# A fused recurrent-attention and two-MoE kernel: low parts of the weights formed on the tensor engine, two-operand GpSimd work moved to the vector engine

## The chip, the cores and the metric

The kernel runs on one core of a Trainium2 chip. A core has five engines that run side by side and wait for each other through semaphores: TensorE (PE in the rows; its weight loads are PEld), VectorE (DVE), ScalarE (ACT), GpSimd (POOL) and SyncE (SP), which only issues transfers here. The metric is the device time of one execution in microseconds, the median of the timed runs. The kernel before took 1139.43 us (three runs, 1137.97 to 1142.35).

## The reference, cut to what matters

```
for t in range(768):                       # 4 batches x 8 heads, state 40 x 40
    y[t]  = r[t] @ state
    Sa    = state @ a[t]
    state = state * w[t] - outer(Sa, b[t]) + outer(v[t], k[t])
x = y as 3072 rows of 320                  # 8 heads x 40
h = x @ w_in                               # 320 -> 2048
g = h if h >= 1, 0 if h <= -1, else (h + 1)**2 / 4
x = g @ w_out                              # 2048 -> 320
h = max(x @ w1, x @ w2, x @ w3)            # 320 -> 768
out = h @ w_out2                           # 768 -> 320
```

The MoE weights arrive as 64-bit floats. The kernel builds a 32-bit float from the two 32-bit words of each, and then splits it into a high part H, rounded to the tensor engine's fast format (fp32r), and a low part L = value - H. The activations are split the same way, so that one product is three fast products: H times H, H times L, L times H.

## The kernel before, in words

**Stages.** The recurrence runs in 24 chunks of 32 time steps over all 32 (batch, head) pairs. `prep` makes, for two chunks at once, running products X of the decay and their reciprocals R, and `front` and `back` work one chunk: scale k, b and a by R and X (tiles KBT and ta), build small triangular matrices LM and invert them (tiles lp, itmp, T, ttr, a long series of small VectorE instructions), solve for U, and update the state Z. Z of one chunk is needed by the next. After every second chunk, `moe1` runs one unit of the first MoE: 256 rows of x through 128 products with w_in (line 810) and 96 with w_out (line 833), with an activation tile q and its parts gH and gL between them. A last stage, `moe2`, runs the second MoE (lines 947 and 973) when the recurrence has ended.

**Weights.** `weights1` brings the weights of the first MoE in 26 pieces through four raw buffers (`raw0` to `raw2` and `raw4`). `narrow` (715 to 719) turns 64 into 32 bits: ScalarE scales the high word into a tile `tmp` and takes its sign, VectorE shifts the low word (717) and joins both (718), and GpSimd or VectorE multiplies by the sign (719). `split` copies H on ScalarE (737) and subtracts on VectorE or GpSimd (738). The tiles `tmp` are the two q tiles of the MoE and one more. gH, gL and the second pair of x tiles are given the place of the raw buffers by `gates` (762 to 769), which comes when the pieces are done. The second MoE's weights are narrowed between the chunks (`pieces`) and kept in DRAM until `phase2` splits them.

**Order.** Nothing is ordered by hand. Every step is a task with one or more engines it may run on and a duration in ns for each. `Plan.run` puts the tasks on the engines by priority, along a clock of its own made of these durations, and the instructions are written out in that order; each engine then runs its queue strictly in order. Where a task names two engines, the one that would finish it first in the plan, with a constant added for each engine (1500 ns for VectorE, 0 for GpSimd), gets it. Where the plan leaves TensorE without work, `emit` writes products nobody reads (lines 359 and 1000, here called fillers) into a free PSUM bank.

Of the kernel before, what the change touches and what calls it, by code (L numbers as in the profile page):

```python
# [244 lines left out]
def dve(n):  # L245
    return 68 + n / 0.96
# [6 lines left out]
def pool(n):  # L253
    return 98 + n * 2.2
# [11 lines left out]
class Kernel:  # L266
# [46 lines left out]
    def setup_attn(self):  # L313
# [5 lines left out]
        self.mask = ap.tile([128, 7, 32], F32, name="mask")  # L319
        self.delta = ap.tile([128, 4], F32, name="delta")  # L320
# [46 lines left out]
    def prep(self, p):  # L367
# [9 lines left out]
        eng = lambda n: (("DVE", dve(n)),) if p == 0 else (("POOL", 720.0 if n == 128 else pool(n)), ("DVE", dve(n)))  # L377
        P.add((("POOL", 400.0), ("DVE", 150.0)) if p else (("DVE", 150.0),), lambda e: self.copy(e, blk(X, 0), blk(wt, 0)), r=wk, w=xk)
# [4 lines left out]
        P.add((("POOL", 330.0), ("DVE", 120.0)) if p else (("DVE", 120.0),), lambda e: self.copy(e, cum[:, :, 0:3], X[:, :, 8:25:8]), r=xk, w=ck)  # L383
# [58 lines left out]
    def front(self, c):  # L442
# [7 lines left out]
        RX = (("POOL", pool(1024)), ("DVE", dve(1024))) if c > 1 else (("DVE", dve(1024)),)  # L450
        AX_ = (("POOL", pool(512)), ("DVE", dve(512))) if c > 1 else (("DVE", dve(512)),)
# [52 lines left out]
        def op(n, fn, r, w):  # L504
            P.add((("DVE", dve(n) + 100),), fn, r=r, w=w)
# [186 lines left out]
    def setup_moe1(self):  # L692
# [15 lines left out]
    def narrow(self, raw, tmp, n, rk, tk):  # L708
# [31 lines left out]
    def weights1(self):  # L740
# [49 lines left out]
    def moe1(self, u):  # L790
# [6 lines left out]
        for mp in range(8):  # L797
# [23 lines left out]
            P.add((("POOL", pool(512)), ("DVE", dve(512)))[u == 11:], lambda e, q=q, j=j: self.tt(e, self.gL[j], q, self.gH[j].bitcast(F32), ALU.subtract),  # L821
# [54 lines left out]
    def phase2(self):  # L876
# [6 lines left out]
        for k, (_, n) in enumerate(self.pieces2):  # L883
# [3 lines left out]
            if k < 18:  # L887
# [4 lines left out]
                if kt < 2:  # L892
                    P.add((("DVE", dve(n)), ("POOL", pool(n))), lambda e, src=src, j=j, kt=kt, cs=cs: self.tt(e, tl["w3"][:, j, 2 + kt, cs], src(), tl["w3"][:, j, kt, cs].bitcast(F32), ALU.subtract),
                          r=[("tmp2", i), ("w3", j, kt, x)], w=[("w3", j, 2 + kt, x)])
                else:
                    P.add((("DVE", dve(n)), ("POOL", pool(n))), lambda e, src=src, j=j, cs=cs: self.tt(e, tl["w3"][64:128, j, 4, cs], src()[64:128], tl["w3"][64:128, j, 4, cs].bitcast(F32), ALU.subtract),
                          r=[("tmp2", i)], w=[("w3", j, 4, x)])
            else:
                m = k - 18
                P.add((("ACT", act(n)),), lambda e, src=src, m=m: self.copy(e, tl["wo2"][:, m, 0], src()), r=[("tmp2", i)], w=[("wo2", m, 0)])  # L900
                P.add((("DVE", dve(n)), ("POOL", pool(n))), lambda e, src=src, m=m: self.tt(e, tl["wo2"][:, m, 1], src(), tl["wo2"][:, m, 0].bitcast(F32), ALU.subtract),
# [287 lines left out]
def constants():  # L1189
# [9 lines left out]
        "ident": np.eye(128, dtype=np.float32),  # L1199
        "mask": np.stack([lower, two(k, b), two(k, b), lower, two(b, k), two(b, k), two(k, k)], 1),  # L1200
# [54 lines left out]
```

## Time and profile before

| | us |
|---|---|
| median of three runs | 1139.43 (1137.97 to 1142.35) |
| the profiled execution, device time | 1135.63 |
| its span, first to last instruction | 1133.8 |
| TensorE busy in the span | 1050.0 |
| VectorE busy | 660.7 |
| ScalarE busy | 489.4 |
| GpSimd busy | 435.7 |

The span has four stretches: the start, in which the weights come in and the first two chunks run (0 to 127 us); the chunks with the first MoE's units between them (127 to about 840); a short passage; and the second MoE (from 860 on). Busy time of TensorE is modelled for pipelined products and says little about how near it is to its best. A duration of a VectorE row reaches from its start to its end and can overlap the next by some 0.08 us.

### The profile page before, as it was taken

The numbers are of one execution on the slowest core, as the hardware profiler recorded it, in microseconds if no ns is written. First come the engines' busy times: TensorE is split into PE (matmuls) and PEld (weight loads), VectorE is DVE, ScalarE is ACT, GpSimd is POOL, SyncE is SP. The second block draws the span as 40 slices with busy tenths as digits, with TensorE's granted clock in tenths as the row PEclk, the third lists the DMA queues.
The fourth block names the chain that finished last, engine by engine and source line by source line (L and its number), as shares of the span: only waits on it lengthen the run. The fifth ranks groups of instructions, "written<-read, shape, count | busy, mean of one in ns | idle before, by whom it ended". The sixth has DMA issues, their size and how long they took to land.

```text
span 1133.8 us, 50184 instructions
## 1 busy us (share of the span) xinstructions
PE 1050.0 (93%) x22708; PEld 948.5 (84%) x22708; DVE 660.7 (58%) x1509; ACT 489.4 (43%) x1137; POOL 435.7 (38%) x478
## 2 busy tenths in 40 slices
PE   6888799999999999998999989999999999999996
PEld 6877789888888888887888878888998888888885
DVE  7989968576684939577483938555244333332321
ACT  3465355545554444544445353445564212222121
POOL 4979642356654545355545525522134000000000
PEclk9799899899999999999999999999999999999998
DMA  8444231313332222322121211200053101100000
GB/s 221 126 142 124 85 107 49 95 54 92 99 90 84 76 76 56 103 60 75 51 59 31 55 43 36 62 26 24 4 157 111 40 12 52 34 18 24 1 24 27
DMA packets 42866, 76.66 MB, mean 68 GB/s; under 512 B 8820, under 2 KB 24436, under 8 KB 42644
## 3 DMA queue, kind: packets, MB, share of 16 engines
q1 hardware_dynamic: 42500, 73.31, 22.9%
q8 instruction: 180, 2.95, 1.1%
q14 instruction: 42, 0.34, 0.1%
q10 hardware_dynamic: 144, 0.07, 0.0%
HBM read 60.96 MB, written 12.39 MB: 65 GB/s over the span
## 4 chain that ended last, share of the span: by engine, by line
PE 75%; DVE 11%; ACT 4%; issue 4%; DMA 4%; POOL 0%; SPq 0%; DVEq 0%; ACTq 0%; POOLq 0%
PE bank L947 18%; PE bank L810 15%; PE bank L833 12%; PE bank L973 6%; PE bank L1000 5%; PE bank L585 3%; PE bank L562 3%; PE bank L577 2%; DVE Z L301 2%; PE bank L666 2%; PE bank L479 2%; PE bank L432 2%; PE bank L652 2%; DMA KBT<-in_kbT 2%; ACT VU L289 1%
## 5 line engine op out<-in xcount | busy, mean ns | idle before, releaser
L833 PE MATMUL bank<-wo,gH 128*128 128x320 f32 x768 | 181.7, 323 | 0.0
L810 PE MATMUL bank<-xH,wi 128*128 128x256 f32 x960 | 160.7, 298 | 1.1 <-issue 1.1
L301 POOL TENSOR_TENSOR gL<-q,gH 128x512 fp32r<-128x512 f32 x86 | 110.8, 1291 | 123.5 <-ACT gH L281 92.9
L817 ACT ACTIVATE q<-bank,half 128x512 f32<-128x512 f32 x96 | 66.0, 688 | 165.8 <-PE bank L810 154.5
L810 PEld LDWEIGHTS bank<-xH,wi 128*128 128x128 f32 x960 | 131.4, 195 | 5.3 <-issue 1.3
L819 DVE SCALAR_TENSOR_TENSOR q<-bank,q 128x512 f32<-128x512 f32 x96 | 65.8, 685 | 107.8 <-ACT q L818 88.8
L833 PEld LDWEIGHTS bank<-wo,gH 128*128 128x128 f32 x768 | 125.3, 191 | 2.7
L833 PE MATMUL bank<-wo,gL 128*128 128x320 f32 x384 | 119.5, 311 | 0.0
L810 PE MATMUL bank<-xL,wi 128*128 128x256 f32 x576 | 103.0, 288 | 7.5 <-DVE xL L301 4.6
L947 PE MATMUL bank<-wi,w 128*128 128x512 f32 x432 | 102.7, 396 | 0.0
L1000 PE MATMUL bank<-ident 128*128 128x128 bf16 (+2 forms) x1194 | 88.3, 233 | 9.1 <-DVE LM L301 6.7
L947 PEld LDWEIGHTS bank<-wi,w 128*128 128x128 f32 x432 | 80.8, 188 | 18.6
L810 PEld LDWEIGHTS bank<-xL,wi 128*128 128x128 f32 x576 | 84.9, 196 | 8.6 <-DVE xL L301 5.4
L1000 PEld LDWEIGHTS <-ident 128*128 128x128 bf16 x1194 | 77.6, 102 | 13.8 <-issue 9.2
L301 DVE TENSOR_TENSOR q<-s,bank 128x512 f32<-128x512 f32 x36 | 24.8, 688 | 83.8 <-PE bank L947 83.1
L833 PEld LDWEIGHTS bank<-wo,gL 128*128 128x128 f32 x384 | 73.0, 190 | 0.1
L281 ACT CAST gH<-q 128x512 fp32r<-128x512 f32 x96 | 59.0, 615 | 27.7 <-PE bank L833 20.0
L947 PE MATMUL bank<-yH,w 128*128 128x512 f32 x270 | 70.5, 391 | 0.4 <-DVE wi L301 0.4
L281 ACT CAST wi<-s 128x512 fp32r<-128x512 f32 x36 | 22.5, 625 | 109.0 <-DVE s L301 109.0
L973 PE MATMUL bank<-wo,wi 128*128 128x320 f32 x432 | 66.0, 309 | 0.0
L973 PEld LDWEIGHTS bank<-wo,wi 128*128 128x128 f32 x432 | 64.7, 188 | 1.4
L301 POOL TENSOR_TENSOR R<-R,wT 104x128 f32<-104x128 f32 x74 | 56.1, 759 | 19.1 <-DVE R L388 5.7
(145 smaller groups left out, 2057.1 us busy)
## 6 DMA issues: line engine op xcount, KB each, us to landing
KBT<-in_kbT SPq DMA_DIRECT2D x24, 416.0 KB
raw<-in_moe_w_out SPq DMA_DIRECT2D x22, 320.0 KB
VU<-in_vn SPq DMA_DIRECT2D x96, 64.0 KB
wT<-in_wT SPq DMA_DIRECT2D x12, 429.0 KB
ta<-in_aT SPq DMA_DIRECT2D x24, 208.0 KB
tr<-in_rT SPq DMA_DIRECT2D x24, 208.0 KB
raw<-in_moe_w SPq DMA_DIRECT2D x12, 384.0 KB
raw<-in_moe_w_in SPq DMA_DIRECT2D x8, 512.0 KB
```

The lines of the kernel that those rows point to most:

```text
L281: self.nc.scalar.copy(out, in_)
L301: (self.nc.vector if eng == "DVE" else self.nc.gpsimd).tensor_tensor(*a)
L432: nc.tensor.transpose(p[:, m * 104:(m + 1) * 104], src(m), self.ident[0:104, 0:104])
L562: nc.tensor.matmul(self.bank[gs[x].bank][ts, o + j * D:o + (j + 1) * D], t[lo:hi, j, ts], z(lo, hi, bb, j), start=(opens and j == 0), stop ...
L585: nc.tensor.matmul(self.bank[g1[q].bank][us, o:o + D], self.ttr[QS[bb], h].rearrange("p i q -> p (i q)"), ru[QS[bb], h, :], start=(first a ...
L810: nc.tensor.matmul(p, a, b, start=(i == 0), stop=(i == 7))
L817: P.add((("ACT", act(512)),), lambda e, q=q, bv=bv: nc.scalar.activation(q, bv(), AF.Relu, bias=self.half, scale=0.5), w=[("q", j)], g=[g])
L819: P.add((("DVE", dve(512)),), lambda e, q=q, bv=bv: nc.vector.scalar_tensor_tensor(q, bv(), 1.0, q, ALU.max, ALU.min), w=[("q", j)], g=[g])
L833: nc.tensor.matmul(p, a, b, start=(m == 0 and i == 0), stop=(m == 15 and i == 2))
L947: nc.tensor.matmul(p, a, b, start=(i == 0), stop=(i == 7))
L973: nc.tensor.matmul(p, a, b, start=(m == n == 0), stop=(m == 5 and n == 2))
L1000: nc.tensor.matmul(self.bank[b][:, 0:n], w[:, 0:128], w[:, 0:n], start=True, stop=True)
```

## The change

- `split` no longer subtracts. A new function `rest` lets TensorE add the value times the identity and H times minus the identity in a PSUM bank of class "h" (banks 4 and 5, which the first MoE's units use later), and ScalarE copies the sum to L. The constant minus1 is one more input, loaded on ScalarE's queue ahead of ident.
- `narrow` writes to three tiles of their own; q is no longer used for it, gH and gL have their place from the beginning, and `gates` (now `others`) only makes the second x tiles. In exchange there are two raw buffers and raw4 instead of three and raw4.
- All two-operand work that could go to GpSimd is now VectorE's alone: X, R and their copies in `prep`, KBT and ta in `front`, the sign product in `narrow`, gL in `moe1`, the low parts in `phase2`. GpSimd keeps the constant on lp's diagonal, copies of WCT, and the squares of q where the plan gives them to it.
- Two durations of the plan change: the small steps of the inversion from +100 to +20 ns, the shift in `narrow` from +250 to +0.

```
-        eng = lambda n: (("DVE", dve(n)),) if p == 0 else (("POOL", 720.0 if n == 128 else pool(n)), ("DVE", dve(n)))
+        eng = lambda n: (("DVE", dve(n)),)
...
-        RX = (("POOL", pool(1024)), ("DVE", dve(1024))) if c > 1 else (("DVE", dve(1024)),)
-        AX_ = (("POOL", pool(512)), ("DVE", dve(512))) if c > 1 else (("DVE", dve(512)),)
+        RX = (("DVE", dve(1024)),)
+        AX_ = (("DVE", dve(512)),)
...
-            P.add((("DVE", dve(n) + 100),), fn, r=r, w=w)
+            P.add((("DVE", dve(n) + 20),), fn, r=r, w=w)
...
+        self.gH, self.gL = (t([128, 2, 256], n, 2, F32R) for n in ("gH", "gL"))
...
-        self.raw = [rp.tile([128, 1024], F32, name=f"raw{i}") for i in range(3)]
-        self.tmp = [x.rearrange("p a b -> p (a b)") for x in self.q] + [rp.tile([128, 512], F32, name="tmp")]
+        self.raw = [rp.tile([128, 1024], F32, name=f"raw{i}") for i in range(2)]
+        self.tmp = [rp.tile([128, 512], F32, name=f"tmp{i}") for i in range(3)]
...
-        P.add((("DVE", dvc(n) + 250),), lambda e: nc.vector.tensor_scalar(lo, lo, 29, None, ALU.logical_shift_right), w=rk)
+        P.add((("DVE", dvc(n)),), lambda e: nc.vector.tensor_scalar(lo, lo, 29, None, ALU.logical_shift_right), w=rk)
...
-        P.add((("POOL", pool(n)), ("DVE", dve(n))), lambda e: self.tt(e, tmp, tmp, sg, ALU.mult), r=rk, w=[tk])
+        P.add((("DVE", dve(n)),), lambda e: self.tt(e, tmp, tmp, sg, ALU.mult), r=rk, w=[tk])
...
-        P.add((("DVE", dve(n)), ("POOL", pool(n))), lambda e: self.tt(e, L_, st, H_.bitcast(F32), ALU.subtract), r=[sk, hk], w=[lk])
+        self.rest(st, H_, L_, n, [sk, hk], lk)
+
+    def rest(self, st, H_, L_, n, rk, lk):
+        nc, P = self.nc, self.P
+        g = Group("h")
+        def diff(e):
+            p = self.bank[g.bank][0:128, 0:n]
+            nc.tensor.matmul(p, self.ident, st, start=True, stop=False)
+            nc.tensor.matmul(p, self.minus1, H_.bitcast(F32), start=False, stop=True)
+        P.add((("PE", n * 3.6),), diff, r=rk, g=[g], k=8)
+        P.add((("ACT", act(n)),), lambda e: self.copy(e, L_, self.bank[g.bank][:, 0:n]), w=[lk], g=[g])
...
-            P.add((("POOL", pool(512)), ("DVE", dve(512)))[u == 11:], lambda e, q=q, j=j: self.tt(e, self.gL[j], q, self.gH[j].bitcast(F32), ALU.subtract),
+            P.add((("DVE", dve(512)),), lambda e, q=q, j=j: self.tt(e, self.gL[j], q, self.gH[j].bitcast(F32), ALU.subtract),
```

The order of VectorE in the middle of the recurrence, from the transposition that ends one chunk's inversion (ttr) to the state update (Z). Before:

```order
L534 STREAM_TRANSPOSE ttr_139<-T_136 128x32x8
L301 TENSOR_TENSOR gL_2431<-q_83,gH_2429 128x512
L717 TENSOR_SCALAR raw_142<-raw_142 128x384
L718 SCALAR_TENSOR_TENSOR raw_142<-raw_142 128x384
L301 TENSOR_TENSOR Z_128<-bank_67,Z_128 104x2x4x40
L301 TENSOR_TENSOR Z_128<-bank_68,Z_128 104x2x4x40
L301 TENSOR_TENSOR Z_128<-Z_128,WCT_130 104x2x4x40 x2
L819 SCALAR_TENSOR_TENSOR q_82<-bank_71,q_82 128x512
```

The same stretch of VectorE's queue, of a like pair of chunks, in the changed kernel:

```order
L301 TENSOR_TENSOR ta_122<-ta_122,X_114 104x512
L301 TENSOR_TENSOR R_116<-R_116,wT_112 104x128
L301 TENSOR_TENSOR raw_149<-raw_149 128x384
L536 STREAM_TRANSPOSE ttr_146<-T_143 128x32x8
L396 TENSOR_REDUCE lim_148<-cum_118 104x1 x2
L301 TENSOR_TENSOR KBT_120<-KBT_120,R_116 104x1024
L301 TENSOR_TENSOR gL_87<-q_83,gH_85 128x512
L301 TENSOR_TENSOR Z_135<-bank_67,Z_135 104x2x4x40
L301 TENSOR_TENSOR Z_135<-bank_70,Z_135 104x2x4x40
L301 TENSOR_TENSOR Z_135<-Z_135,WCT_137 104x2x4x40 x2
L834 SCALAR_TENSOR_TENSOR q_82<-bank_72,q_82 128x512
```

The products of ta, R, raw and KBT, which stood on GpSimd, now stand in VectorE's queue; those of ta and KBT follow a transfer. Between the transposition of lp of chunk 4 and that of chunk 6 VectorE had 103 instructions and has 140; up to that of chunk 2 it had 196 and has 231.

TensorE in the start, around the transposition of VU and the state product (KBn) of the first chunk. Before:

```order
L652 MATMUL bank_69<-ident,VU_123 128x128 x4
L652 MATMUL bank_70<-ident,VU_123 128x128 x4
L1000 LDWEIGHTS ident
L1000 MATMUL bank_71<-ident 128x128
...
L634 MATMUL bank_69<-VU_123,KBn_119 40x40
L634 MATMUL bank_70<-VU_123,KBn_119 40x40
```

The same place in the changed kernel:

```order
L654 MATMUL bank_68<-ident,VU_130 128x128 x4
L654 MATMUL bank_67<-ident,VU_130 128x128 x4
L750 MATMUL bank_72<-tmp_93,ident 128x320
L751 MATMUL bank_72<-wo_79,minus_106 128x320
L636 MATMUL bank_68<-VU_130,KBn_126 40x40
L636 MATMUL bank_67<-VU_130,KBn_126 40x40
```

The two products of a piece's low part stand where 31 fillers stood. Ahead of the first product of the first MoE there were 982 fillers and are 332, and all but a few of the 24 low parts; from there to the second MoE there were 212 fillers of 256 columns and are 84, and 4 short ones.

## Rows read from the trace of the kernel before

**Rows 1.** Busy time by stretch: TensorE, its loads, VectorE, ScalarE, GpSimd, granted clock, DMA, GB/s
```profile
0.00:127.00 127.00, 98.95 (x2749) 91.95 (x2749) 115.86 (x213) 60.51 (x139) 94.91 (x104) 0.88 0.55 151
150.00:810.00 660.00, 615.60 (x17823) 561.52 (x17821) 421.70 (x1072) 325.20 (x794) 300.94 (x332) 0.98 0.23 64
810.00:860.00 50.00, 49.38 (x469) 46.47 (x468) 22.18 (x36) 31.02 (x62) 19.04 (x18) 1.00 0.44 129
860.00:1134.00 274.00, 263.08 (x1327) 226.99 (x1325) 81.88 (x123) 61.72 (x118) 6.99 (x8) 0.99 0.10 28
```

**Rows 2.** The chain that ended last, shares of the span by engine
```profile
PE 75%; DVE 11%; ACT 4%; issue 4%; DMA 4%; POOL 0%; SPq 0%; DVEq 0%; ACTq 0%; POOLq 0%
```

**Rows 3.** VectorE's groups by form: busy us, mean ns of one, idle before
```profile
L301 DVE TENSOR_TENSOR Z<-Z,WCT 104x320 f32<-104x320 f32 x46 | 39.8, 895 | 0.0
L301 DVE TENSOR_TENSOR Z<-bank,Z 104x320 f32<-104x320 f32 x46 | 20.6, 481 | 34.2 <-PE bank L634 32.0 <-ACT raw L716 2.3
L526 DVE TENSOR_TENSOR itmp<-T,lp 128x16 f32<-128x16 f32 (+1 forms) x144 | 52.9, 405 | 0.3
L529 DVE TENSOR_REDUCE ir<-itmp 128x4 f32<-128x16 f32 (+1 forms) x144 | 26.9, 222 | 0.0
L530 DVE TENSOR_TENSOR itmp<-ir,lp 128x16 f32<-128x16 f32 (+1 forms) x144 | 44.1, 340 | 0.0
L510 DVE TENSOR_TENSOR itmp<-lp 128x16 f32<-128x16 f32 x24 | 14.4, 598 | 0.3
```

**Rows 4.** Timeline of VectorE and GpSimd at 118 us: start us, us
```profile
118.19 3.48 DVE L718 SCALAR_TENSOR_TENSOR q<-q,raw 128x320 uint32<-128x320 uint32 x2
118.73 2.58 POOL L301 TENSOR_TENSOR KBT<-KBT,R 104x1024 f32<-104x1024 f32 x1
```

**Rows 5.** VectorE's own price of moved forms: tile gL (min/median/max ns), timeline of the start
```profile
L301 DVE TENSOR_TENSOR gL<-q,gH x10: 678/692/2415, 400.0 to 856.2; 128x512 fp32r<-128x512 f32 x10
...
6.05 2.98 DVE L301 TENSOR_TENSOR X<-X,wT 104x128 f32<-104x128 f32 x7
...
19.90 0.38 DVE L301 TENSOR_TENSOR R<-R,wT 104x128 f32<-104x128 f32 x1
20.20 0.48 DVE L718 SCALAR_TENSOR_TENSOR q<-q,raw 128x320 uint32<-128x320 uint32 x1
```

**Rows 6.** The chain in order of time, dense stretches: start us, us
```profile
451.85 0.94 PE bank L810 x8
452.79 0.71 PE bank L562 x57
453.50 1.14 PE bank L810 x8
...
477.99 1.07 PE bank L666 x64
...
829.48 3.52 PE bank L833 x24
833.00 2.83 PE bank L810 x24
```

**Rows 7.** VectorE's timeline: the transposition of lp of chunks 2 and 22
```profile
115.78 2.00 DVE L492 STREAM_TRANSPOSE lp<-LM 128x1024 f32<-128x1024 f32 x1
...
746.51 2.04 DVE L492 STREAM_TRANSPOSE lp<-LM 128x1024 f32<-128x1024 f32 x1
```

**Rows 8.** The chain: a transfer and fillers in the start, products of line 810 at 216
```profile
17.64 8.49 DMA raw<-in_moe_w_out
...
42.51 16.13 PE bank L1000 x263
...
216.04 2.01 PE bank L810 x8
```

**Rows 9.** Who waited for whom: us in total, times, longest
```profile
DVE q L819 <- ACT q L818: 88.8, 43, 6.5
POOL ta L301 <- DMA ta<-in_aT: 52.9, 14, 7.5
DVE LM L301 <- PE bank L479: 32.3, 9, 7.3
DVE Z L301 <- PE bank L634: 32.0, 11, 5.5
POOL KBT L301 <- DMA KBT<-in_kbT: 22.1, 7, 7.9
```

More of the change, by code (lines that the diff above doesn't have):

```diff
@@ L376, in prep @@
         blk = lambda t, i: t[:, :, i:i + 25:8]
-        eng = lambda n: (("DVE", dve(n)),) if p == 0 else (("POOL", 720.0 if n == 128 else pool(n)), ("DVE", dve(n)))
-        P.add((("POOL", 400.0), ("DVE", 150.0)) if p else (("DVE", 150.0),), lambda e: self.copy(e, blk(X, 0), blk(wt, 0)), r=wk, w=xk)
+        eng = lambda n: (("DVE", dve(n)),)
+        P.add((("DVE", 150.0),), lambda e: self.copy(e, blk(X, 0), blk(wt, 0)), r=wk, w=xk)
         for i in range(1, 8):
@@ L382, in prep @@
             P.add(eng(256), lambda e, k=k: self.tt(e, X[:, :, k:k + 8], X[:, :, k:k + 8], X[:, :, k - 1:k].to_broadcast([104, 32, 8]), ALU.mult), w=xk)
-        P.add((("POOL", 330.0), ("DVE", 120.0)) if p else (("DVE", 120.0),), lambda e: self.copy(e, cum[:, :, 0:3], X[:, :, 8:25:8]), r=xk, w=ck)
+        P.add((("DVE", 120.0),), lambda e: self.copy(e, cum[:, :, 0:3], X[:, :, 8:25:8]), r=xk, w=ck)
         P.add(eng(32), lambda e: self.tt(e, cum[:, :, 3:4], X[:, :, 31:32], wt[:, :, 32:33], ALU.mult), r=wk + xk, w=ck)
@@ L401, in pieces @@
             for rows, src in srcs:
-                P.add((("SP", 450.0),), lambda e, rows=rows, src=src, n=n: nc.sync.dma_start(flat.bitcast(U32)[rows, 0:2 * n], src.bitcast(U32)), w=[("raw", 3)], size=1024 * n)
-            self.narrow(flat[:, 0:2 * n], flat[:, 768:768 + n], n, [("raw", 3)], "flat")
-            P.add((("SP", 450.0),), lambda e, k=k, n=n: nc.sync.dma_start(self.w2d[k][:, 0:n], flat[:, 768:768 + n]), r=[("raw", 3), "flat"], w=[("w2d", k)], size=512 * n)
+                P.add((("SP", 450.0),), lambda e, rows=rows, src=src, n=n: nc.sync.dma_start(flat.bitcast(U32)[rows, 0:2 * n], src.bitcast(U32)), w=[("raw", 2)], size=1024 * n)
+            self.narrow(flat[:, 0:2 * n], flat[:, 768:768 + n], n, [("raw", 2)], "flat")
+            P.add((("SP", 450.0),), lambda e, k=k, n=n: nc.sync.dma_start(self.w2d[k][:, 0:n], flat[:, 768:768 + n]), r=[("raw", 2), "flat"], w=[("w2d", k)], size=512 * n)
     def slot(self, h):
@@ L760, in weights1, with others @@
                 self.split(io["moe_w_out"][m * 128:(m + 1) * 128, :], DM, wo[:, m, 0], wo[:, m, 1], ("wo", m, 0), ("wo", m, 1))
-        P.add((("SP", 1.0),), lambda e: self.gates(), w=[("raw", i) for i in range(3)] + ["tmp"] + [(n, j) for n in ("gH", "gL") for j in range(2)] + [(n, 1, c) for n in ("xH", "xL") for c in range(2)])
-    def gates(self):
+        P.add((("SP", 1.0),), lambda e: self.others(), w=[("raw", i) for i in range(2)] + [("tmp", i) for i in range(3)] + [(n, 1, c) for n in ("xH", "xL") for c in range(2)])
+    def others(self):
         self.rctx.close()
-        gp = self.ctx.enter_context(self.tc.tile_pool(name="gates", bufs=1, side="right"))
-        self.gH, self.gL = ([gp.tile([128, 2, 256], F32R, name=f"{n}{i}") for i in range(2)] for n in ("gH", "gL"))
+        gp = self.ctx.enter_context(self.tc.tile_pool(name="others", bufs=1, side="right"))
         for x, n in ((self.xH, "xH1"), (self.xL, "xL1")):
@@ L900, in phase2 @@
                 P.add((("ACT", act(n)),), lambda e, src=src, m=m: self.copy(e, tl["wo2"][:, m, 0], src()), r=[("tmp2", i)], w=[("wo2", m, 0)])
[L901 removed]
+                P.add((("DVE", dve(n)),), lambda e, src=src, m=m: self.tt(e, tl["wo2"][:, m, 1], src(), tl["wo2"][:, m, 0].bitcast(F32), ALU.subtract),
                       r=[("tmp2", i), ("wo2", m, 0)], w=[("wo2", m, 1)])
```

13 lines of the change are left out of this document (8 added, 5 removed).

## The prediction

> **What bounds the kernel now.** I read the busy times by stretch first, then the chain of waits, then VectorE's groups by form, and last the chain in order of time.
>
> By stretch [rows 1] there are three regimes. In the start VectorE is busy 115.86 of 127 us and sets the pace. From 150 to 810 TensorE is busy 615.60 of 660, though modelled, with VectorE at 421.70. After 860 TensorE never stops, and VectorE is at 81.88 of 274. The chain [rows 2] is TensorE for 75% and VectorE for 11%, some 125 us of the 1133.8.
>
> VectorE's groups [rows 3] show what part of that is not work. The update of Z with both operands in SBUF takes 895 ns on average, the one of the same size with an operand in PSUM 481. Line 526 takes 405 ns, line 529, which reduces what 526 has just written, 222. The reduction has one operand, the product two. The timeline shows why [rows 4]: two joins of line 718, for which 0.48 us apiece is normal [rows 5], lasted 3.48 us while GpSimd ran one product of 2.58 us. A two-operand instruction of VectorE is held up by one of GpSimd. Four groups [rows 3] give a lower bound for it: 46 x (895 - 481) = 19.0 us, 144 x (405 - 222) = 26.4, 144 x (340 - 222) = 17.0, 24 x (598 - 222) = 9.0, together 71 us. The joins and the other small lines come on top; I take 90 us over the 810 us in which GpSimd works.
>
> In the middle two chunks and a unit of the first MoE take (746.51 - 115.78) / 10 = 63.1 us [rows 7]; I call this a pair. TensorE's own need in one, from dense stretches of the chain [rows 6]: 128 products of line 810 at 2.83 / 24 = 0.118 us and 96 of line 833 at 3.52 / 24 = 0.147 make 29.2; the bursts of a chunk (some 16, of 0.71 to 1.07 for the products with small tiles, the transpositions less) add up to about 12.1, so 24.2 for two; and a block of eight of line 810 behind a burst takes 1.14 instead of 0.94, so 0.2 for each of some 26 blocks, 5.2. Sum 58.6. The remaining 4.5 us of a pair are waits and fillers; that is all the middle can give, 10.5 pairs x 4.5 = 47 us.
>
> **The change part by part.** The sum stands against the profiled execution, 1135.6 us; the median of the runs is 3.8 higher, so the forecast of the median is moved by that.
>
> *GpSimd's work on VectorE.* It removes the 90 us of holding up and adds the work itself. A pair gets 140 - 103 = 37 instructions more. Prices [rows 5]: gL at 512 columns 0.69 us; X, seven in 2.98, so 0.43 each when each waits for the last; R 0.38, after which the next starts at 0.30. So 37 instructions cost 11 (at 0.30) to 25 us (at 0.69); most are X and R, so I take 0.45 and 17 us. VectorE in a pair: 421.70 / 660 x 63.1 = 40.3 now, less 90 x 63.1 / 810 = 7, plus 17: 50 of 63. It stays below TensorE's 58.6.
>
> [...]
>
> *The middle.* With the holding up gone, Z, the inversion and gL (two engine changes less) come when the plan has them. VectorE keeps 13 us of slack in a pair, and will at times still be late, so I give back 3.5 of the 4.5 us: 10.5 x 3.5 = 37 us. Bounds: 47 (all), and below zero the rival of VectorE's queue. That only 88 fillers stand there instead of 212 is part of this, not a further term.
>
> *The start.* GpSimd is busier here, 94.91 of 127 against 300.94 of 660 [rows 1], so of the 90 us I put 90 x 87 / (87 + 192) = 28 here, each stretch's VectorE time weighted by GpSimd's share. VectorE gets 231 - 196 = 35 instructions more, at 0.45 some 16 us. Net 12 us earlier. Bounds: 28 earlier (what is added is hidden), 42 later (the third rival below).
>
> *Low parts on TensorE.* 24 pieces, 8 of 512 and 16 of 320 columns, two products each. The trace has no full fp32 product of this shape. From below: the fast format's 0.147 us for 320 columns [rows 6], so 8 x 2 x 0.235 + 16 x 2 x 0.147 = 8.5 us. From above: the 3.6 ns per column that the diff gives the plan, 8 x 1.84 + 16 x 1.15 = 33 us. In the same stretch 650 fillers go, at 16.13 / 263 = 0.061 us [rows 8] 40 us. So it costs nothing while the pieces are there in time; if not, the whole queue of TensorE stands behind the product, since it takes its work in order. ScalarE gets 24 copies of at most 0.7 us, 17 us, and is busy only 60.51 of 127.
>
> *Own tiles.* gH, gL and q no longer wait for the last piece; the products of line 833 may start with the first unit. The weights have three raw buffers instead of four. Together I count them at nothing, with the rival below as the bound.
>
> *The passage and the end.* From 810 to 860 GpSimd's 18 instructions at no more than 0.69 us come to VectorE, 12 us on 22.18 of 50: hidden. From 860 on nothing changes, as TensorE is fed and VectorE idle by two thirds. Zero for both.
>
> Sum: 12 + 37 = 49 us less, 1135.6 - 49 = 1086.6, and as a median 1139.4 - 49 = 1090.
>
> **The rivals** (as medians).
>
> *Everything fed.* The start gains its 28 us, the middle its 47: 1139.4 - 75 = 1064. For it: VectorE's slack of 13 us and the fillers that go. Against: two engines above 80%, each waiting for the other in a strict order.
>
> *Only the start gains.* What VectorE takes over delays it in the middle as much as GpSimd did: 1139.4 - 12 = 1127. For it: 17 us come and 7 go in a pair.
>
> *VectorE's queue becomes the bound: slower.* GpSimd now waits 52.9 us for ta's transfers and 22.1 for KBT's [rows 9]; in the new order these products stand in VectorE's queue ahead of gL and Z, so an unfinished transfer holds the state update. A pair's VectorE time would be 50, plus (52.9 + 22.1) / 10.5 = 7.1, plus what it waits today for TensorE before LM and Z, (32.3 + 32.0) / 12 = 5.4, plus its waits for ScalarE's q, 88.8 / 12 = 7.4: 69.9 if none of them overlap. It decides once this passes 63.1; halfway, 3.4 us a pair, it costs 36 us, and the start gains nothing: 1175. Against: the order puts 10 to 20 instructions between, and waits overlap.
>
> *The weights come late.* 26 pieces go through four buffers in about 127 us, a round of 19.5 us for each buffer; a transfer alone takes 8.49 [rows 8]. Were the round to stay, three buffers need 169 us: 42 us later, 1139.4 - 37 + 42 = 1144. Against: most of the round is VectorE's and GpSimd's delay.
>
> [...]
>
> **How the numbers follow.** Chances: forecast 0.42 (its own range 1072 to 1108), everything fed 0.20, only the start 0.15, VectorE's queue 0.11, late weights 0.06, clock 0.06. The range 1050 to 1140 holds the forecast, the start alone, the clock, most of everything fed and part of the late weights, some 0.82. About 0.5%, 5.7 us, can be told from no change. Faster by more: 0.42 + 0.20 + 0.14 + 0.04 + 0.01 = 0.81; within: 0.01 + 0.01 + 0.03 = 0.05; slower: 0.11 + 0.01 + 0.02 = 0.14.
>
> **What would show it.** Right: lines 508 to 530's products within 20% of the reductions beside them; Z's two updates alike, near 0.48; lp of chunk 2 transposed near 104 us; a pair near 59.6; from the passage on the same 274 us. VectorE in the middle at 75 to 85% of the stretch. Wrong: VectorE idle behind transfers of KBT or ta with Z queued behind; TensorE waiting at a low part's product; a granted clock below 0.95 in the middle; a pair still at 63.

## The result, and the profile after

The changed kernel takes 1092.87 us, median of four runs (1089.28 to 1102.01), beside 1140.6 (1137.97 to 1142.35) for the kernel before on the same chip: a ratio of 0.9598, 95% interval 0.9555 to 0.9641. The profiled execution took 1090.74 us, its span is 1089.0.

The page of the profile after: busy time of each engine, and the chain that ended last, by engine. They answer to the busy times of before and to [rows 2].

```profile
PE 1023.9 (94%) x22030; PEld 906.7 (83%) x22030; DVE 712.6 (65%) x1906; ACT 500.1 (46%) x1153; POOL 26.4 (2%) x65
...
PE 75%; DVE 11%; ACT 4%; DMA 4%; issue 4%; SPq 0%; ACTq 0%; DVEq 0%
```

GpSimd goes from 435.7 to 26.4 us, and VectorE, which took its work, only from 660.7 to 712.6. The shares of the chain are those of before: the chain became shorter in about the same proportion everywhere, and no engine took it over.

Busy time by stretch in the profile after, columns as in [rows 1]; the third row ends ahead of the second MoE, which now begins at 805.5.

```profile
0.00:127.00 127.00, 106.38 (x2464) 81.97 (x2465) 106.81 (x320) 77.27 (x181) 6.06 (x17) 0.95 0.54 144
150.00:810.00 660.00, 627.66 (x17533) 573.71 (x17532) 500.34 (x1415) 346.76 (x820) 19.32 (x47) 0.99 0.26 72
150.00:770.00 620.00, 587.66 (x17233) 534.63 (x17231) 475.62 (x1370) 318.65 (x765) 19.32 (x47) 0.99 0.24 68
```

In the start VectorE issues 320 instructions where it issued 213, in less busy time (106.81 against 115.86). In the middle it is busy 475.62 of 620 us, 77%. The granted clock is higher in both stretches, 0.95 and 0.99 instead of 0.88 and 0.98; what that may be worth stands under the clock below.

VectorE's groups of the profile after, the answers to [rows 3] (same lines, shifted: 528, 531, 532 and 512 were 526, 529, 530 and 510) and the main groups that GpSimd had: busy us, mean ns, idle before.

```profile
L301 DVE TENSOR_TENSOR Z<-Z,WCT 104x320 f32<-104x320 f32 x46 | 21.9, 502 | 0.0
L301 DVE TENSOR_TENSOR Z<-bank,Z 104x320 f32<-104x320 f32 x46 | 21.1, 483 | 5.7 <-PE bank L636 5.6
L528 DVE TENSOR_TENSOR itmp<-T,lp 128x16 f32<-128x16 f32 (+1 forms) x144 | 27.6, 231 | 0.2
L531 DVE TENSOR_REDUCE ir<-itmp 128x4 f32<-128x16 f32 (+1 forms) x144 | 26.6, 224 | 0.0
L532 DVE TENSOR_TENSOR itmp<-ir,lp 128x16 f32<-128x16 f32 (+1 forms) x144 | 21.4, 186 | 0.0
L512 DVE TENSOR_TENSOR itmp<-lp 128x16 f32<-128x16 f32 x24 | 4.0, 169 | 0.1
...
L301 DVE TENSOR_TENSOR gL<-q,gH 128x512 fp32r<-128x512 f32 x96 | 65.5, 683 | 24.6 <-ACT gH L281 24.4
L301 DVE TENSOR_TENSOR R<-R,wT 104x128 f32<-104x128 f32 x84 | 34.3, 408 | 0.3
L301 DVE TENSOR_TENSOR X<-X,wT 104x128 f32<-104x128 f32 x84 | 33.9, 405 | 2.2
L301 DVE TENSOR_TENSOR KBT<-KBT,R 104x1024 f32<-104x1024 f32 x24 | 29.2, 1220 | 5.3 <-DMA KBT<-in_kbT 4.3 <-PE bank L848 1.0
```

The two updates of Z now cost the same, and line 528's product costs what the reduction behind it does. What VectorE took over it does in about half of GpSimd's time (gL 683 ns against 1291, KBT 1220 against 2501).

VectorE's timeline after: the transposition of lp of chunks 2 and 22, as in [rows 7], and TensorE's first product of the second MoE.

```profile
102.58 1.98 DVE L494 STREAM_TRANSPOSE lp<-LM 128x1024 f32<-128x1024 f32 x1
...
712.38 1.96 DVE L494 STREAM_TRANSPOSE lp<-LM 128x1024 f32<-128x1024 f32 x1
...
805.53 1.32 PE L962 MATMUL bank<-yH,w 128*128 128x512 f32 x5
```

These place the 44.8 us of span. Up to lp of chunk 2: 115.78 - 102.58 = 13.2 us. The ten pairs from there: 630.7 against 609.8, 20.9 us, 60.98 us a pair. From lp of chunk 22 to the first product of the last unit (818.0 before, 774.8 now): 9.1. From there to the second MoE (850.6 and 805.5): 1.9. The second MoE takes 283.2 and 283.5 us.

Who waited for whom after: us in total, times, longest; the answers to [rows 9].

```profile
DVE q L834 <- ACT q L833: 40.4, 24, 5.0
DVE ta L301 <- DMA ta<-in_aT: 27.7, 12, 4.2
...
DVE Z L301 <- PE bank L636: 5.6, 4, 3.1
DVE LM L301 <- PE bank L481: 5.4, 4, 2.5
...
DVE KBT L301 <- DMA KBT<-in_kbT: 4.3, 6, 1.3
```

VectorE's waits for TensorE ahead of LM and Z fell from 64 to 11 us. The transfers of ta and KBT, for which GpSimd waited 75 us, hold VectorE for 32.

### The profile page after: what moved, and what is told of

Its sections match the earlier page's. It is cut to its first block, busy times and chain, and to the rows that moved or that the text cites. A ratio compares the mean times of both kernels' runs of the same rounds, so it can differ in the third digit from the quotient of the medians.

```text
span 1089.0 us, 48670 instructions
## 1 busy us (share of the span) xinstructions
PE 1023.9 (94%) x22030; PEld 906.7 (83%) x22030; DVE 712.6 (65%) x1906; ACT 500.1 (46%) x1153; POOL 26.4 (2%) x65
## 4 chain that ended last, share of the span: by engine, by line
PE 75%; DVE 11%; ACT 4%; DMA 4%; issue 4%; SPq 0%; ACTq 0%; DVEq 0%
PE bank L962 18%; PE bank L825 14%; PE bank L848 13%; PE bank L988 6%; PE bank L579 3%; PE bank L587 3%; PE bank L564 2%; PE bank L434 2%; ACT VU L289 2%; PE bank L668 2%; PE bank L481 2%; PE bank L654 2%; PE bank L1015 2%; DVE X L301 1%; DMA raw<-in_moe_w_out 1%
## 5 line engine op out<-in xcount | busy, mean ns | idle before, releaser
L848 PE MATMUL bank<-wo,gH 128*128 128x320 f32 x768 | 184.3, 325 | 3.1 <-issue 3.1
L825 PE MATMUL bank<-xH,wi 128*128 128x256 f32 x960 | 156.2, 292 | 4.3 <-issue 4.2
L825 PEld LDWEIGHTS bank<-xH,wi 128*128 128x128 f32 x960 | 127.7, 189 | 8.9 <-issue 5.0
L825 PE MATMUL bank<-xL,wi 128*128 128x256 f32 x576 | 99.5, 281 | 0.3 <-issue 0.2
L825 PEld LDWEIGHTS bank<-xL,wi 128*128 128x128 f32 x576 | 81.7, 189 | 0.7 <-issue 0.4
L301 DVE TENSOR_TENSOR gL<-q,gH 128x512 fp32r<-128x512 f32 x96 | 65.5, 683 | 24.6 <-ACT gH L281 24.4
L301 DVE TENSOR_TENSOR s<-q,bank 128x512 f32<-128x512 f32 x36 | 24.8, 688 | 63.9 <-PE bank L962 63.9
L289 ACT ACTIVATE VU<-bank 32x160 f32<-32x160 f32 x192 | 52.8, 293 | 16.6 <-PE bank L587 14.2
L962 PEld LDWEIGHTS bank<-yH,w 128*128 128x128 f32 x270 | 50.1, 188 | 9.7
```

Of the source, the lines that this page charges most:

```text
L289: self.nc.scalar.activation(out, in_, AF.Copy, scale=-1.0)
L301: (self.nc.vector if eng == "DVE" else self.nc.gpsimd).tensor_tensor(*a)
L825: nc.tensor.matmul(p, a, b, start=(i == 0), stop=(i == 7))
L848: nc.tensor.matmul(p, a, b, start=(m == 0 and i == 0), stop=(m == 15 and i == 2))
L962: nc.tensor.matmul(p, a, b, start=(i == 0), stop=(i == 7))
```

## The experiments

Each kernel is compared with the kernel before on its own chip, so ratios are compared and not times. The expectations give times, and mean the chip of the result, where the kernel before takes 1140.6 us; on the other chips it took 1130.8 to 1138.4. A time is therefore also given "put on the first chip", as the ratio times 1140.6. The table has the ratio and its interval, and from the profiled execution of each the three places used above, in us: the transposition of lp of chunk 2, a pair (lp of chunk 2 to 22, by ten), the first product of the last unit of the first MoE. Each place is that of a single execution; the runs of one kernel differ by up to 1.3%, and in the changed kernel and every variant but raw_both the longest had a lower granted clock than the shortest (weights_only took 1115.43 us at 0.980 and 1129.98 at 0.970), so differences of half a microsecond in a pair say little.

| kernel | ratio | interval | chunk 2 | pair | last unit |
|---|---|---|---|---|---|
| before | 1 | | 115.8 | 63.07 | 818.0 |
| changed | 0.9598 | 0.9555 to 0.9641 | 102.6 | 60.98 | 774.8 |
| weights_only | 0.9911 | 0.9870 to 0.9952 | 111.6 | 63.82 | 814.1 |
| engines_only | 0.9754 | 0.9697 to 0.9812 | 126.3 | 61.00 | 796.2 |
| no_rest | 0.9721 | 0.9666 to 0.9776 | 123.1 | 60.11 | 785.7 |
| old_costs | 0.9753 | 0.9697 to 0.9810 | 107.5 | 61.01 | 786.8 |
| gp_reads | 0.9797 | 0.9721 to 0.9872 | 105.3 | 62.48 | 791.0 |
| gp_writes | 0.9617 | 0.9537 to 0.9697 | 103.0 | 60.66 | 771.4 |
| no_gl_vector | 0.9509 | 0.9424 to 0.9593 | 104.1 | 59.40 | 767.1 |
| no_gl_tensor | 0.9269 | 0.9197 to 0.9341 | 103.5 | 58.39 | 738.6 |
| raw_three | 0.9565 | 0.9492 to 0.9637 | 102.2 | 60.42 | 765.8 |
| raw_lim | 0.9687 | 0.9645 to 0.9729 | 103.6 | 61.73 | 781.0 |
| raw_both | 0.9535 | 0.9503 to 0.9566 | 104.9 | 60.66 | 772.2 |
| raw_sq | 0.9612 | 0.9568 to 0.9656 | 101.2 | 62.17 | 784.7 |

**One part alone: weights_only and engines_only.** The first keeps the new way of the weights and gives GpSimd's options and the old durations back:

```
-        eng = lambda n: (("DVE", dve(n)),)
+        eng = lambda n: (("DVE", dve(n)),) if p == 0 else (("POOL", 720.0 if n == 128 else pool(n)), ("DVE", dve(n)))
...
-            P.add((("DVE", dve(n) + 20),), fn, r=r, w=w)
+            P.add((("DVE", dve(n) + 100),), fn, r=r, w=w)
```

> The weights' part of the change alone: low parts on TensorE, own tiles, two raw buffers and raw4; GpSimd keeps its two-operand work and the plan its old durations. Theory A (the gain comes from VectorE no longer being held up by GpSimd): the middle stays at 62.8 us from one MoE unit to the next, only the start may come some us earlier; 1128 to 1140 us. Theory B (the weights' part makes the gain, above all in the start): the first MoE unit begins some 20 us before 127, the time is 1120 or less.

Measured 1124.02 us against 1134.12. Put on the first chip that is 1130, in A's band; as a bare time it lies between the two. The pair, 63.8, did not get shorter, and chunk 2 came 4.2 us earlier, as A has it. The second is the kernel before with all of that changed and the weights as they were, low parts on VectorE:

```
-        P.add((("DVE", dve(n)), ("POOL", pool(n))), lambda e: self.tt(e, L_, st, H_.bitcast(F32), ALU.subtract), r=[sk, hk], w=[lk])
+        P.add((("DVE", dve(n)),), lambda e: self.tt(e, L_, st, H_.bitcast(F32), ALU.subtract), r=[sk, hk], w=[lk])
```

> The engines' part alone: all two-operand work of GpSimd on VectorE and the two new durations; weights as before, with the low parts subtracted on VectorE. Theory A: units 61 us apart in the middle and the start 10 to 15 us earlier, 1100 to 1110 us. Theory B: the middle gains its 21 us at most, the start nothing, since VectorE now has the subtractions as well: 1120 or more.

Measured 1107.24 against 1134.12, in A's band; put on the first chip, 1113, it lies between the bands and nearer to A's. A's pair came, its earlier chunk 2 did not. The pair is what the engines decide: 61.0 us with GpSimd's work on VectorE, 63.8 without. The start needs both parts: with the engines alone chunk 2 comes 10.5 us later than before, though the units of the first MoE begin at 105.7 instead of 127.0.

**The low parts back on VectorE: no_rest.**

```
-        self.rest(st, H_, L_, n, [sk, hk], lk)
+        P.add((("DVE", dve(n)),), lambda e: self.tt(e, L_, st, H_.bitcast(F32), ALU.subtract), r=[sk, hk], w=[lk])
```

> The changed kernel, but the low parts of the first MoE's weights are subtracted on VectorE instead of summed on TensorE. 24 subtractions, 8 of 512 and 16 of 320 columns at 0.68 and 0.48 us, are 13 us more on VectorE in the start; 48 products, about 32 us, and 24 copies of ScalarE go. Theory A (the start runs at VectorE's pace, and TensorE has room there): first product of line 825's like 5 to 13 us later than the 104.6 us of the changed kernel, lp of chunk 2 later as well, ratio to the kernel before 0.964 to 0.974. Theory B (the low parts on TensorE cost on the chain what VectorE saves): within 4 us of the changed kernel's 0.960.

Measured 1101.79 against 1133.89, a ratio in the band of A. VectorE's groups for it up to 140 us, and its timeline:

```profile
L301 DVE TENSOR_TENSOR wo<-tmp,wo 128x320 fp32r<-128x320 f32 x16 | 7.6, 487 | 1.6 <-ACT wo L281 1.6
L301 DVE TENSOR_TENSOR wi<-tmp,wi 128x512 fp32r<-128x512 f32 x8 | 5.5, 690 | 5.0 <-ACT wi L281 5.0
```

```profile
123.14 1.98 DVE L494 STREAM_TRANSPOSE lp<-LM 128x1024 f32<-128x1024 f32 x1
```

With these 24 subtractions, 13.1 us of VectorE, chunk 2 comes 20.6 us later, of which 10.9 are left at the last unit; why it is more than 13.1 is not shown. The first unit begins at 104.4, as in the changed kernel (104.6): A's 5 to 13 us later did not come, and taking the 48 products off TensorE brought it no earlier.

**The plan's durations: old_costs.**

```
-            P.add((("DVE", dve(n) + 20),), fn, r=r, w=w)
+            P.add((("DVE", dve(n) + 100),), fn, r=r, w=w)
...
-        P.add((("DVE", dvc(n)),), lambda e: nc.vector.tensor_scalar(lo, lo, 29, None, ALU.logical_shift_right), w=rk)
+        P.add((("DVE", dvc(n) + 250),), lambda e: nc.vector.tensor_scalar(lo, lo, 29, None, ALU.logical_shift_right), w=rk)
```

> The changed kernel with the plan's two durations as they were (+100 and +250 ns); the work is the same, only the order differs. If the gain is work and waits: within 8 us of 1093. If it is the order that the new durations give: 1105 or more.

Measured 1104.9 against 1134.12; put on the first chip that is 1112, in the band of the order. It is 1.5% above the changed kernel's ratio with the same work in another order: VectorE has 1906 instructions in both, two squares of q went from GpSimd to ScalarE, and TensorE has 213 records more, which are fillers. Its four runs had a granted clock of 0.976 to 0.980, the changed kernel's 0.976 to 0.987. The pair is the same, 61.0; 4.9 us are lost ahead of chunk 2 and some 7 between chunk 22 and the last unit.

**What holds VectorE up: gp_reads and gp_writes.** GpSimd does idle work that touches a tile of its own, in each chunk 24 products of the tile with itself, or 44 fills of it:

```
+        z, last = self.idle, P.tasks[-1]
+        for _ in range(24):
+            P.add((("POOL", 0.1),), lambda e, z=z: nc.gpsimd.tensor_tensor(z, z, z, ALU.mult), w=["idle"], after=[last])
```
```
+        for _ in range(44):
+            P.add((("POOL", 0.1),), lambda e, z=z: nc.gpsimd.memset(z, 0.0), w=["idle"], after=[last])
```

> The changed kernel, with 24 products of a 128x128 tile of zeros with itself put on GpSimd behind each chunk's constant on lp's diagonal, some 9 us a chunk, nobody waits for them; they run while VectorE inverts. All other queues keep their order. Theory A (a two-operand instruction of VectorE is held up while GpSimd reads): lines 510 to 532's products rise from 0.17 to 0.30 us to 0.4 and more, VectorE gets 60 to 100 us busier, the time goes back by 15 us or more, to 1108 to 1135. Rival (the extra time of before was VectorE waiting for other things): nothing, 1093 within 5.

> The same with 44 fills of the tile instead of the products, as long for GpSimd, which write and read nothing. If only GpSimd's reads hold VectorE up: 1093 within 5, lines 510 to 532 as in the changed kernel. If any work of GpSimd does: like the run with products.

Measured 1108.61 and 1087.98 against 1130.8; put on the first chip these are 1117, in A's band, and 1097, in that of reads alone. VectorE's groups with GpSimd reading (gp_reads; lines 533, 536, 537 and 517 are 528, 531, 532 and 512 of the changed kernel):

```profile
L301 DVE TENSOR_TENSOR Z<-Z,WCT 104x320 f32<-104x320 f32 x46 | 24.8, 567 | 0.0
L301 DVE TENSOR_TENSOR Z<-bank,Z 104x320 f32<-104x320 f32 x46 | 21.4, 494 | 0.9 <-PE bank L641 0.9
L533 DVE TENSOR_TENSOR itmp<-T,lp 128x16 f32<-128x16 f32 (+1 forms) x144 | 36.0, 287 | 0.2
L536 DVE TENSOR_REDUCE ir<-itmp 128x4 f32<-128x16 f32 (+1 forms) x144 | 26.5, 222 | 0.0
L517 DVE TENSOR_TENSOR itmp<-lp 128x16 f32<-128x16 f32 x24 | 6.5, 272 | 0.1
```

The same groups with GpSimd only writing (gp_writes):

```profile
L301 DVE TENSOR_TENSOR Z<-Z,WCT 104x320 f32<-104x320 f32 x46 | 21.9, 504 | 0.0
L301 DVE TENSOR_TENSOR Z<-bank,Z 104x320 f32<-104x320 f32 x46 | 21.1, 484 | 4.7 <-PE bank L641 4.7
L533 DVE TENSOR_TENSOR itmp<-T,lp 128x16 f32<-128x16 f32 (+1 forms) x144 | 27.7, 231 | 0.2
L536 DVE TENSOR_REDUCE ir<-itmp 128x4 f32<-128x16 f32 (+1 forms) x144 | 26.7, 225 | 0.0
L517 DVE TENSOR_TENSOR itmp<-lp 128x16 f32<-128x16 f32 x24 | 4.1, 170 | 0.1
```

GpSimd's own groups, in gp_reads and in gp_writes:

```profile
L503 POOL TENSOR_TENSOR idle<-idle 128x128 f32<-128x128 f32 x576 | 297.6, 517 | 43.2
```

```profile
L503 POOL MEMSET idle<- 128x128 f32 x1056 | 217.9, 206 | 59.1
```

With 298 us of reads the groups above with two operands in SBUF are longer (567, 287 and 272 ns instead of 502, 231 and 169), the reduction and the update from PSUM are hardly so (222 and 494 ns beside 224 and 483), VectorE is busy 749.0 us instead of 712.6, and the kernel loses half of what the change gained. A's direction is right and its sizes are not: it expected 0.4 us and more for the small products (0.23 to 0.29 came) and 60 to 100 us more for VectorE (36.4 came). With 218 us of fills none of these groups is longer by more than 2 ns (504, 231 and 170, 225 and 484), VectorE is busy 712.7 us and nothing is lost. So what held VectorE's two-operand instructions up here was GpSimd's products, which read SBUF, and not its fills, which only write it (line 533: 287 ns in the kernel with the products, 231 in that with the fills).

**What bounds the middle: no_gl_vector and no_gl_tensor.** The first drops VectorE's subtraction and lets TensorE multiply gH in its place, the second drops TensorE's 384 products of gL:

```
-            P.add((("DVE", dve(512)),), lambda e, q=q, j=j: self.tt(e, self.gL[j], q, self.gH[j].bitcast(F32), ALU.subtract),
-                  r=[("q", j), ("gH", j)], w=[("gL", j)])
```
```
-                        seq = [(gH[:, mm, ts], wo[:, m, 0]), (gH[:, mm, ts], wo[:, m, 1]), (gL[:, mm, ts], wo[:, m, 0])]
+                        seq = [(gH[:, mm, ts], wo[:, m, 0]), (gH[:, mm, ts], wo[:, m, 1])]
```

> The changed kernel without VectorE's gL (96 subtractions, 65 us of VectorE); TensorE multiplies gH in its place, so its work stays. What it leaves out: the low part of the first MoE's activations. If the middle is bound by TensorE: 1093 to 1083. If by VectorE: 5 us less per unit, 1035 to 1045. If the two hold each other: 1060 to 1080.

> The changed kernel without TensorE's products of gL (384 at 0.147 us, 56 us of TensorE); VectorE still makes gL. What it leaves out: the same low part. If the middle is bound by TensorE: 4.7 us less per unit, 1035 to 1045. If by VectorE: 1083 to 1093. If the two hold each other: 1050 to 1075.

Measured 1079.14 and 1050.78 against 1130.8; put on the first chip, 1085 and 1057. The second lies in the band of two engines that hold each other, the first in that band as a time and in TensorE's on the first chip. In a pair 8 x 0.683 = 5.5 us less on VectorE bring 1.6 us; 32 x 0.147 = 4.7 us less on TensorE [rows 6] bring 2.6, and from the first product of the last unit, which has no chunk beside it, to the second MoE it is 20.6 us instead of 30.7. TensorE decides more, neither decides alone. The sizes are those of single executions: in the ten pairs TensorE ran at a granted clock of 0.50 for 23.8 us without VectorE's gL, 17.0 without TensorE's products and 6.8 in the changed kernel, and at an equal clock both answers would be larger, an estimate from half of these being 2.4 and 3.1 us.

**Buffers: raw_three.** Three raw buffers and raw4, and two of the three tiles `tmp` in the place of q, as before; gH and gL keep their own:

```
-        self.raw = [rp.tile([128, 1024], F32, name=f"raw{i}") for i in range(2)]
-        self.tmp = [rp.tile([128, 512], F32, name=f"tmp{i}") for i in range(3)]
+        self.raw = [rp.tile([128, 1024], F32, name=f"raw{i}") for i in range(3)]
+        self.tmp = [x.rearrange("p a b -> p (a b)") for x in self.q] + [rp.tile([128, 512], F32, name="tmp")]
```

> The changed kernel with three raw buffers and raw4 again; to make room two of the three narrow tiles are the q tiles, as before. If the start waits for weights that come late through too few buffers: first MoE unit 5 to 10 us earlier, 1083 to 1088 us. If own tiles are what brought the start forward: the first unit waits for the q tiles, 1095 to 1110 us.

Measured 1085.31 against 1134.12; put on the first chip that is 1091, between the two bands. The first unit begins at 99.7 instead of 104.6 and the last 9.0 us earlier; but the intervals of the two ratios overlap, so that what own tiles and two buffers cost or bring is not told from zero here.

**An attempt to go further: raw_lim, raw_both, raw_sq.** All three start from raw_three. raw_lim splits a long reduction, raw_sq takes the squares of q from GpSimd, raw_both does both:

```
-            P.add((("DVE", dve(1024)),), lambda e, x=x, op=op: nc.vector.tensor_reduce(self.lim[0:104, x, 2 * p:2 * p + 1], X, axis=AX.XY, op=op), r=xk, w=[("lim", x, 2 * p)])
+            for s in range(4):
+                P.add((("DVE", dve(256)),), lambda e, x=x, op=op, s=s: nc.vector.tensor_reduce(self.lim[0:104, x, 5 * p + s:5 * p + s + 1], X[:, :, 8 * s:8 * s + 8], axis=AX.XY, op=op), r=xk, w=[("lim", x, 5 * p + s)])
```
```
-            P.add((("ACT", act(512)), ("POOL", pool(512))), lambda e, q=q: nc.scalar.square(q, q) if e == "ACT" else self.tt(e, q, q, q, ALU.mult), w=[("q", j)])
+            P.add((("ACT", act(512)),), lambda e, q=q: nc.scalar.square(q, q) if e == "ACT" else self.tt(e, q, q, q, ALU.mult), w=[("q", j)])
```

> Three raw buffers and raw4 as in raw_three, and each of the 24 reductions of X over 1024 columns (1.21 us on VectorE, 11 us of them on the chain of the changed kernel in the middle) is made as four of 256, so that none holds the queue for 1.2 us. Theory A (what stands on the chain there is one long instruction ahead of an urgent one): 4 to 8 us faster than raw_three, ratio to the kernel before 0.948 to 0.953. Theory B (VectorE's total counts, and the order of the queue is strict): as raw_three, 0.955 to 0.960, since the sum of the four is no shorter than the one.

> raw_lim, and the squares of q on ScalarE alone, so that GpSimd reads next to nothing any more. Theory A (GpSimd's squares, some 30 of 1.3 us, are late for VectorE, which waits 8 us for them in the changed kernel): 3 to 6 us faster than raw_lim. Theory B (ScalarE, which makes the squares instead and is waited for 108 us by itself for TensorE's products, becomes later by as much): the same as raw_lim within 3 us.

> raw_three with the squares of q on ScalarE alone; the reductions of X are whole again. raw_lim (whole minus split) measured 0.969, raw_both (split, squares on ScalarE) 0.954, raw_three 0.957. Theory A (the squares themselves are worth the 17 us between raw_lim and raw_both): 0.94 to 0.946. Theory B (the reductions and the squares move each other in the plan, and what a small edit moves is the order, worth some 1% either way): 0.950 to 0.960, and the lp of chunk 2, the pair and the last unit each move by a few us without a common sign.

Measured 1099.14 and 1081.42 against 1133.89, and 1098.86 against 1138.4. raw_lim fell outside both bands, since it is slower than raw_three by 1.2%; the four reductions cost 4 x 0.411 us where the one cost 1.21, some 10 us more of VectorE's work, but raw_both has these too and is the lowest of the four. raw_both came out 17.7 us below raw_lim, more than A's 3 to 6. raw_sq came out just above B's band and far from A's, so the squares are not worth 17 us; its own runs spread from 1087.45 us (granted clock 0.991) to 1100.99 (0.979), and its interval overlaps that of raw_three. So the split alone made the kernel slower, the squares alone changed nothing that is clear of noise, and with both together it is as fast as raw_three. That these edits work by the order in which the plan puts all the rest is what is left as a reading, and is not shown by itself; old_costs, with the same work, is the cleaner measure of that, 1.5%. raw_both's ratio, 0.9535, is the lowest that any version with the full computation reached, 0.6% under the changed kernel's, and their intervals still touch.

## Why the prediction was right, and where its terms were off

**The sum.** 49 us were forecast and 44.9 came, from one profiled execution to the other; 1090 as a median, 1092.87 measured. The likeliest case was the one that happened, though part of the gain may have come by a way that the sum did not hold, the clock (below).

**GpSimd's holding up of VectorE** was the right mechanism: gp_reads and gp_writes show it by itself (VectorE busy 36.4 us more beside 298 us of products, 0.1 beside 218 us of fills), and the trace of before shows how (last section). The term of 90 us was too small. The four groups that gave 71 us give 2 now (46 x 19 ns and 144 x 7 ns; the other two cost less than the reduction). An estimate for the whole: the instructions that VectorE took over, at their means after, make some 207 us (86 of gL 58.7, 74 of R 30.2, 71 of X 28.8, 18 of KBT 22.0, the rest, smaller groups, 67), less some 32 for 400 starts that lie 0.08 us ahead of the last one's end [rows 5]; VectorE's busy time rose by 51.9, so about 123 us of holding up went. A count in the trace of before comes to the same: its 291 VectorE instructions with two operands in SBUF that had a product of GpSimd beside them took 122 us longer than the same forms do on average after, and the 324 that had none 1 us less.

**VectorE's load.** Forecast 50 us of a pair, measured 475.62 / 620 x 60.98 = 46.8; the mis-sized 90 us makes most of the difference: 123 instead of 90 is 2.6 us of a pair.

**The start.** Forecast 12 us, measured 13.2 to chunk 2. What makes this possible stands in the sum only unspoken, in the 35 instructions that it took from the new order: GpSimd formed 23 of the 24 low parts before, in some 25 us, and with GpSimd's work moved these would have been VectorE's. The prediction counted TensorE's products as a cost that fillers cover, and did not say what they keep off VectorE; no_rest puts that at 20.6 us of the start and 1.2% of the kernel.

**Low parts on TensorE.** The bounds were 8.5 to 33 us, taken as nothing since fillers cover it. The chain after, around two pieces that stand on it:

```profile
59.93 0.55 PE bank L654 x5
60.48 0.54 PE bank L750 x2
61.02 0.54 PE bank L751 x2
61.56 0.76 PE bank L636 x64
62.31 1.06 PE bank L750 x2
63.37 0.87 PE bank L751 x2
```

Line 750 and line 751 are the two products of a piece, 320 columns in the first two rows and 512 in the last two (each shows as two records). A piece takes 1.08 or 1.93 us, so that 24 at these prices make 16 x 1.08 + 8 x 1.93 = 32.7: the upper bound. Two of them ran at a granted clock of 0.50, from 33.75 and from 39.75, and took 2.43 each, which makes it 35.4. "It costs nothing" is too strong: nine of the 24 stand on the chain, 11% of its first 130 us. The first unit of no_rest, which comes no earlier without them, shows that they cost no more than the subtractions that they replace.

**The middle** is the term that was too large: 37 us were forecast, and from chunk 2 to the last unit 30.0 came, 20.9 in the ten pairs and 9.1 in the last. The step that failed is "I give back 3.5 of the 4.5 us": a pair gave 2.1. It took TensorE's sum, 58.6, as the floor, and VectorE's 13 us of slack as enough to reach it; and of the 4.5 us, which it called waits and fillers, some 1.5 were the lower clock (half of the 30.6 us that the ten pairs had at a granted clock of 0.50, an estimate). The two kernels without gL show that the pair answers to both engines, by about a third of what VectorE loses and by half of what TensorE loses, though VectorE is idle for 14 us of it; both shares are rough, as said there. The chain runs through both in turn, and slack elsewhere doesn't help the instruction that is on it. How much of the remaining 2.4 us a better order could give isn't settled: kernels with GpSimd's work on VectorE that differ in small things have pairs from 60.1 to 62.2.

**Passage and end.** Zero was forecast for both; 1.9 us came off the passage, and the second MoE took 0.3 more.

**The rivals.** VectorE's queue did not become the bound: the transfers of ta and KBT hold it 32 us, and it waits 11 for TensorE at Z and LM. The weights do come late at places. The chain after, in the start:

```profile
71.06 5.02 DMA raw<-in_moe_w_in
...
100.49 4.93 DMA raw<-in_moe_w_out
```

and the third buffer moved the first unit by 4.9 us; that is far from the 42 of the rival.

**The clock** has no term in the sum of the forecast; the prediction gives its fall a chance of 0.06 and counts a granted clock below 0.95 in the middle as a sign of being wrong. No run shows that fewer fillers lower it, and here it rose, with 88 fillers instead of 212: the granted clock of the profiled execution is 0.972 before and 0.987 after. Busy time by stretch, columns as in [rows 1], from lp of chunk 2 to that of chunk 22 before, then 10 us ahead of a stretch at the lower of the two levels that the trace shows, 0.50 and 1.00, and that stretch:

```profile
115.78:746.51 630.73, 584.08 (x16762) 533.16 (x16760) 419.20 (x1063) 307.01 (x751) 308.97 (x344) 0.98 0.24 68
206.00:216.00 10.00, 8.12 (x239) 7.07 (x237) 5.47 (x6) 5.97 (x17) 4.76 (x4) 1.00 0.18 46
216.00:222.80 6.80, 6.80 (x123) 6.26 (x120) 0.69 (x1) 0.74 (x4) 2.40 (x3) 0.50 0.55 160
```

From lp of chunk 2 to that of chunk 22 after:

```profile
102.58:712.38 609.80, 577.87 (x16852) 524.61 (x16850) 486.17 (x1396) 318.96 (x767) 20.35 (x47) 0.99 0.26 73
```

From chunk 2 to the last unit TensorE ran at 0.50 for 34.0 us before, in six stretches, and for 6.8 after, in one (from 281.8). Eight products of line 810 take 2.01 us there instead of 0.94 [rows 6, 8], so the 27.2 us less may have given back up to 13.6 of the middle's 30.0, an estimate. The four runs of the changed kernel, with the same instructions, bear the size out: 1089.28, 1090.74, 1095.0 and 1102.01 us at granted clocks of 0.986, 0.987, 0.981 and 0.976, some 11 us for 0.01. TensorE sat idle 4.7 us of a pair before, at a granted clock of 0.98, and 3.2 after, at 0.99; that the one comes of the other is not shown. No run holds the clock and changes the rest, so how much of the gain is the clock's is not shown either.

**What it owed to the order.** Nothing in the prediction said that the two new durations of the plan matter by themselves. old_costs puts them at 1.5%, raw_lim shows another small edit at 1.2%, and the runs of the changed kernel alone spread by 1.2% with the granted clock. The forecast's error of 0.3% is smaller than all of these; the direction and the mechanism were reasoned, the closeness is in part luck.

## What to carry to other kernels

Look in the profile for a two-operand instruction of VectorE and a one-operand one of like size beside it: where the first is longer and GpSimd reads SBUF at the same time (here 405 ns beside 222 before, 231 beside 224 after), GpSimd's help may be paid for by VectorE, and giving the work back can cost less than it seems (here 207 us of work raised VectorE's busy time by 52). When work moves to the engine that sets the pace, take something else off it in the same stretch: each half of this change alone gave 0.9 and 2.5%, both 4.0. Where a planner sets the order, hold an effect of 1% against what a meaningless edit does, and against the granted clocks of the runs, before giving it a cause.

## What the runs showed of the hardware that was not expected

How much GpSimd's products held VectorE up went with their length. In gp_reads products of 0.517 us on average lengthened Z's update by 63 ns; before, it was longer by 414 ns [rows 3]. The update of Z in SBUF before, with min/median/max in ns, and two places of VectorE's and GpSimd's timeline:

```profile
L301 DVE TENSOR_TENSOR Z<-Z,WCT x46: 436/484/2665, 73.3 to 789.2; 104x320 f32<-104x320 f32 x46
...
209.84 1.28 POOL L301 TENSOR_TENSOR gL<-q,gH 128x512 fp32r<-128x512 f32 x1 [3.82 <-ACT gH L281]
210.22 3.83 DVE L301 TENSOR_TENSOR Z<-Z,WCT 104x320 f32<-104x320 f32 x2
211.08 2.62 POOL L301 TENSOR_TENSOR KBT<-KBT,R 104x1024 f32<-104x1024 f32 x1
...
272.85 1.21 DVE L301 TENSOR_TENSOR Z<-Z,WCT 104x320 f32<-104x320 f32 x2
273.72 2.55 POOL L301 TENSOR_TENSOR KBT<-KBT,R 104x1024 f32<-104x1024 f32 x1 [0.41 <-DMA KBT<-in_kbT]
```

At the median an update takes 0.48 us. Ten began while one product of GpSimd was running and had no other beside them; each ended 0.35 us (346 to 352 ns) behind that product's end, whether it was one of 1.0, 1.3 or 2.4 to 2.6 us, as the second of the pair at 210.22 did behind KBT. The second of the pair at 272.85 began 0.14 us ahead of KBT and took 0.48. So each of the ten waited out what was left of the product beside it, and the longest, of 2.67 us, had one of 2.64 beside it. In gp_reads, where half of the products take no more than 0.402 us, little is left: five of nine such updates ended 0.35 to 0.46 us behind the product, and four took 0.49 to 0.51 beside products that had themselves become longer than 1.2 us, so that there the product was the longer one and not the update. GpSimd's reading one tile twice there is not the reason: in the changed kernel one update began beside a square of q, which also reads one tile twice, and took 1.33 us, to 0.35 us behind the square's end.
